# Rewriting a one-core decode-layer forward and backward kernel: program order, 32-bit transposes, longer DMA rows

## The chip, the cores and the metric

The kernel runs on one NeuronCore of a Trainium2 chip. The metric is device time in microseconds (us) of one execution, as the median of several runs. TensorE (PE) multiplies matrices into PSUM, VectorE (DVE) and ScalarE (ACT) copy PSUM to SBUF and do elementwise work, GpSimd (POOL) and SyncE (SP) mostly issue DMAs. Sixteen DMA engines move data between HBM and SBUF; SP, ACT and POOL each issue onto a queue of their own, and all three queues share the sixteen engines.

## The reference

One decode step (batch 4, one query token, model width 512): attention over a sliding window of a K/V cache (32 query heads, 8 K/V heads, head size 128, cache length 4096, window the last 1024 positions) and a gated FFN (width 1792), both from the layer-normed input, and all gradients. Cut to what matters:

```python
W = max(256, Sk // 4)                              # 1024 of 4096 positions
q = (xn @ wq) ; k = k_cache[:, :, Sk-W:] ; v = v_cache[:, :, Sk-W:]
o = softmax(q k^T * Dh**-0.5) v
y = x + o @ wo + (gelu(xn @ w_gate) * (xn @ w_up)) @ w_down
out, vjp = jax.vjp(f, x, k_cache, v_cache, wq, wo, w_gate, w_up, w_down)
return out, *vjp(grad_out)
```

All data are bf16. The gradients of the two caches are 32 MiB each, and three quarters of each is zero (the positions outside the window); these zeros must be written too. Queries in a group of 4 heads share one K/V head, and there is one token per batch, so every product of activations is thin: the large operands are weights and K/V blocks, most of which are wanted transposed.

## The kernel before

The eight K/V heads are handled in four groups `t` of two heads (`GP = 2`). For each group the kernel

- `pre`: transposes `wo` (128x128 bf16 blocks, eight to a PSUM tile, line 258, copied out by DVE on line 92) and forms the output gradient and the queries of its eight query heads by products with 4 moving columns;
- `scores(t, 0)` and `scores(t, 1)`: transposes K, then V, block by block (`T_ps`, line 306), copies them to `T_sb`, and multiplies (`S_ps`, line 311) with four products side by side in 32-column groups of the array (`tile_position`);
- `softmax`, `softmax_d`: the softmax and its derivative;
- `odq`: the attention output and the gradient of q (`od_ps`, line 377);
- `dvdk`: the gradients of V and K as outer products with a contraction of 32 (`kv_ps`, line 406), cast into a staging tile `stg`, and stored;
- `dw`: the gradients of `wo` and `wq`; `fin`: transposes `wq` and adds the group's part of the output and of dx to `acc`.

The FFN comes first, with the same parts: transposes (`wdT_ps`, `wgT_ps`), thin products, and gradients (`dwd_ps`, `dwg_ps`) that are cast into `osb_d` and `osb_g`.

Products whose result is only stored are put into a list `bg` and popped a few at a time by `tick(n)`, between other work. `evac` (lines 91 and 92) gives each PSUM evacuation to ACT or DVE by a running cost balance; bf16 blocks of transposes go to DVE always. The tile framework schedules all engines except SP itself; only SP's queue keeps program order (`manual_schedule(engines={nc.sync.engine})`). PSUM has one pool of four buffers (`ps_w`) for all transposes and products.

DMA: the FFN weights, the first group and part of the second are loaded on SP, the rest on ACT (lines 206, 208, 213). K and V rows: the 1024 positions are split as 128 partitions x 8 positions, so that one descriptor row is 8 x 128 bf16 = 2 KB. `zeros()` issues all 32 zero stores (1536 KB each, 6 KB rows) on SP directly behind its loads; each waits until the one two before it has landed. All gradients are stored from POOL (line 96).

Of the kernel before, what the change touches and what calls it, by code (L numbers as in the profile page):

```python
# [13 lines left out]
BF16 = mybir.dt.bfloat16  # L14
P = 128
# [3 lines left out]
def kernel(  # L19
# [34 lines left out]
    ND = D // P  # L54
    NF = F // P
    J = W // P
# [3 lines left out]
    RG = B * HG  # L60
    NQ = P // RG
    WQ = W // NQ
    JQ = J // NQ
    NS = B * GP
    CW = HG * Dh
    assert Sq == 1 and Dh == P and D == 512 and F % P == 0 and RG == 32 and JQ * NQ == J and WQ == JQ * P
    scale = float(Dh) ** -0.5
    eps = 1e-5

    const = ctx.enter_context(tc.tile_pool(name="const", bufs=1))  # L70
    kvp = ctx.enter_context(tc.tile_pool(name="kvp", bufs=3))
    wres = ctx.enter_context(tc.tile_pool(name="wres", bufs=2))
    attw = ctx.enter_context(tc.tile_pool(name="attw", bufs=2))
    tsb = ctx.enter_context(tc.tile_pool(name="tsb", bufs=5))
    outp = ctx.enter_context(tc.tile_pool(name="outp", bufs=3))
    ps_w = ctx.enter_context(tc.tile_pool(name="ps_w", bufs=4, space=bass.MemoryType.PSUM))
    ps_a = ctx.enter_context(tc.tile_pool(name="ps_a", bufs=1, space=bass.MemoryType.PSUM))
    ps_x = ctx.enter_context(tc.tile_pool(name="ps_x", bufs=1, space=bass.MemoryType.PSUM))
    ctx.enter_context(tc.manual_schedule(engines={nc.sync.engine}))

    load = {"act": 0.0, "dve": 0.0}

    def evac(out, in_, n, half=False, eng=None):

        eng = "dve" if half else eng
        ca, cd = (190 + n) / 1.2, (120 + (n / 2 if half else n)) / 0.96
        if eng is None:
            eng = "act" if load["act"] + ca <= load["dve"] + cd else "dve"
        load[eng] += ca if eng == "act" else cd
        if eng == "act":  # L90
            return nc.scalar.copy(out=out, in_=in_)  # L91
        return nc.vector.tensor_copy(out=out, in_=in_)  # L92

    def store(eng, out, in_, kind, apart):

        d = eng.dma_start(out=out, in_=in_)  # L96
        for k in apart:
            tc.declare_no_dep(d.ins, group=k, reason="stores write disjoint parts of the outputs")
        tc.add_to_no_dep_group(kind, d.ins)
        return d  # L100


    RB = P // B
    x_b = const.tile([P, D], BF16, name="x_b")
    dy_b = const.tile([P, D], BF16, name="dy_b")
    for dst, src in ((x_b, A_x), (dy_b, grad_out)):
        nc.sync.dma_start(out=dst[:], in_=bass.AP(tensor=src.tensor, offset=src.offset,
                                                  ap=[[D, B], [0, RB], [1, D]]))

# [3 lines left out]
    nc.vector.tensor_copy(out=ident_f[:], in_=ident[:])  # L113
    one_f = const.tile([1, 1], FP32, name="one_f")
    nc.vector.memset(one_f[:], 1.0)

    msk_i = const.tile([P, rep], FP32, name="msk_i")
    nc.vector.reduce_sum(out=msk_i[:], in_=ident_f[:].rearrange("p (b r) -> p r b", b=B)[:, 0:rep, :], axis=AX.X)


    rsum = const.tile([P, NQ, RG], FP32, name="rsum")
    nc.gpsimd.memset(rsum[:], 1.0)

    msk_f = const.tile([P, GP, B], FP32, name="msk_f")
    nc.gpsimd.memset(msk_f[:], 1.0)
    for q in range(NQ):
        rs = slice(q * RG, (q + 1) * RG)
        nc.gpsimd.affine_select(out=rsum[rs], in_=rsum[rs], pattern=[[0, NQ], [-1, RG]],
                                compare_op=ALU.is_equal, fill=0.0, base=0, channel_multiplier=1)
        nc.gpsimd.affine_select(out=msk_f[rs], in_=msk_f[rs], pattern=[[-rep, GP], [-HG, B]],  # L130
                                compare_op=ALU.is_ge, fill=0.0, base=0, channel_multiplier=1)
        nc.gpsimd.affine_select(out=msk_f[rs], in_=msk_f[rs], pattern=[[rep, GP], [HG, B]],
                                compare_op=ALU.is_ge, fill=0.0, base=rep - 1, channel_multiplier=-1)
    msk = const.tile([P, GP, B], BF16, name="msk")
    nc.vector.tensor_copy(out=msk[:], in_=msk_f[:])

    ZW = K0 // P * Dh
    ztile = const.tile([P, ZW], BF16, name="ztile")
    nc.vector.memset(ztile[:], 0.0)

    qm_all, dom_all = [], []
    for i in range(2):
        for lst, nm in ((qm_all, "qm"), (dom_all, "dom")):
            t_ = const.tile([P, NS, RG + rep], BF16, name=f"{nm}{i}")
            nc.gpsimd.memset(t_[:], 0.0)
            lst.append(t_)


    acc = const.tile([P, 2, ND, B], FP32, name="acc")
    nc.vector.memset(acc[:], 0.0)  # L150

    def acc_add(o, ps):
        nc.vector.tensor_tensor(out=acc[:, o], in0=ps, in1=acc[:, o], op=ALU.add)

    def acc_sum(o, terms):

        ps = ps_w.tile([P, ND, B], FP32, name="acc_ps", tag="w")
        for c in range(ND):
            for k, (lf, rhs) in enumerate(terms):
                nc.tensor.matmul(ps[:, c, :], lhsT=lf(c), rhs=rhs, start=(k == 0), stop=(k == len(terms) - 1))  # L160
        acc_add(o, ps[:])


    od_ps = ps_a.tile([P, 2, GP, Dh], FP32, name="od_ps")
    nc.vector.memset(od_ps[:], 0.0)


    stats = const.tile([P, nc.vector.BN_STATS_DIM], FP32, name="stats")
    nc.vector.bn_stats(out=stats[:], in_=x_b[:])
    mv = const.tile([P, nc.vector.BN_AGGR_DIM], FP32, name="mv")  # L170
    nc.vector.bn_aggr(out=mv[:], in_=stats[:])
    eps_t = const.tile([P, 1], FP32, name="eps_t")
    nc.vector.memset(eps_t[:], eps)
    rstd = const.tile([P, 1], FP32, name="rstd")
    nc.scalar.activation(out=rstd[:], in_=mv[:, 1:2], func=ACT.Sqrt, bias=eps_t[:], scale=1.0)
    nc.vector.reciprocal(out=rstd[:], in_=rstd[:])
    xn_f = const.tile([P, D], FP32, name="xn_f")
    nc.vector.tensor_scalar(out=xn_f[:], in0=x_b[:], scalar1=mv[:, 0:1], scalar2=rstd[:, 0:1],
                            op0=ALU.subtract, op1=ALU.mult)
    xn_b = const.tile([P, D], BF16, name="xn_b")  # L180
    nc.vector.tensor_copy(out=xn_b[:], in_=xn_f[:])

    xnT = const.tile([P, ND, B], BF16, name="xnT")
    dyT = const.tile([P, ND, B], BF16, name="dyT")
    for src, dstT in ((dy_b, dyT), (xn_b, xnT)):
        tps = ps_x.tile([P, ND, P], BF16, name="tps", tag="x")
        for c in range(ND):
            nc.tensor.transpose(tps[:, c, :], src[:, c * P:(c + 1) * P], ident[:])
        nc.vector.tensor_copy(out=dstT[:], in_=tps[:].rearrange("p c (b r) -> p c b r", b=B)[:, :, :, 0])


    xnm = const.tile([P, rep, D], BF16, name="xnm")
    dym = const.tile([P, rep, D], BF16, name="dym")
    for src, dst in ((dy_b, dym), (xn_b, xnm)):
        for i in range(rep):
            nc.vector.tensor_scalar(out=dst[:, i, :], in0=src[:], scalar1=msk_i[:, i:i + 1], scalar2=None,
                                    op0=ALU.mult)


    wo_v = A_wo.rearrange("(t h p) n -> t p h n", p=P, h=HG)  # L200
    wq_v = A_wq.rearrange("(c p) (t j) -> t p c j", p=P, j=CW)
    wo_t, wq_t, k_t, v_t = {}, {}, {}, {}

    def load_w(t, eng):
        wo_t[t] = wres.tile([P, HG, D], BF16, name="wo_sb", tag="wo")
        eng.dma_start(out=wo_t[t][:], in_=wo_v[t])
        wq_t[t] = wres.tile([P, ND, CW], BF16, name="wq_sb", tag="wq")
        eng.dma_start(out=wq_t[t][:], in_=wq_v[t])  # L208

    def load_kv(t, k, g, eng):  # L210
        d_, src, nm = ((k_t, A_k_cache, "kb"), (v_t, A_v_cache, "vb"))[k]
        tl = kvp.tile([P, B, J, Dh], BF16, name=nm, tag=nm)
        eng.dma_start(out=tl[:].rearrange("p b j d -> p b (j d)"),  # L213
                      in_=src[:, t * GP + g, K0:Sk, :].rearrange("b (m j) d -> m b (j d)", j=J))
        d_[(t, g)] = tl

    def load_next(t, k):

        if t + 1 < NT:
            load_kv(t + 1, k, 1, nc.scalar)  # L220
        if t + 2 < NT:
            load_kv(t + 2, k, 0, nc.scalar)


    ZG = 2
    zlist = [(og, b, g) for b in range(B) for g in range(0, G, ZG) for og in (out_2, out_3)]

    def zeros():
# [14 lines left out]
    def tick(n):  # L243
        for _ in range(min(n, len(bg))):
            bg.popleft()()


    st = {}

# [462 lines left out]
```

## Time and profile before

| | |
|---|---|
| median of 3 runs | 313.86 us (311.71 to 315.93) |
| span of the profiled execution | 311.7 us |
| PE, weight loads | 224.1 us busy (72%), 144.7 us (46%) |
| DVE | 146.3 us (47%) |
| ACT | 113.4 us (36%) |
| POOL | 51.3 us (16%) |
| data moved | 112.38 MB: 30.93 MB read from HBM, 81.01 MB written |
| mean rate over the span | 361 GB/s |

The span is the time from the first to the last instruction of one profiled execution, and its length equals the lowest of the three runs. Busy time of PE is modelled from pipelined instructions. "Mean ns" of a matmul is its latency, and busy time divided by the count is what it costs in a row of its like.

### The profile page before, as it was taken

To read this page: it belongs to the slowest core of one execution; us is meant where nothing else is said; L and a number is where in the kernel's file an instruction comes from. 1 tells how busy PE (TensorE), PEld (TensorE's weight loads), DVE (VectorE), ACT (ScalarE), POOL (GpSimd) and SP (SyncE) were. 2 spreads that over 40 slices of the span, in tenths; PEclk is the share of its full clock that TensorE was granted. 3 is DMA by queue.
4 is the path that set the end of the run, shared out by engine and by line. 5 is a ranking of instruction groups with operands and counts; after the bars stand their busy time and mean duration, and the time that the engine had idled before them with its cause. 6 is when DMAs were issued, how large, how long until landed. Compare 5 with 4: busy or idle time off the path is not lost.

```text
span 311.7 us, 6831 instructions
## 1 busy us (share of the span) xinstructions
PE 224.1 (72%) x2950; PEld 144.7 (46%) x2956; DVE 146.3 (47%) x304; ACT 113.4 (36%) x217; POOL 51.3 (16%) x76
## 2 busy tenths in 40 slices
PE   1269986936988379779648069969789755979861
PEld 0259874615555244465425044455556333756231
DVE  5246663523743234537414025546545424564766
ACT  3010645613613045346022044435244414533650
POOL 6000121610100005201000004201000501110140
PEclk9998998875975555779955555679955559895585
DMA  5999999999999999999999999998999999431494
GB/s 167 397 351 385 374 402 416 416 422 424 419 295 392 418 374 418 421 420 419 375 418 414 357 418 416 421 420 346 394 410 405 418 422 418 159 145 62 181 335 160
DMA packets 34405, 112.38 MB, mean 361 GB/s; under 512 B 1664, under 2 KB 7816, under 8 KB 34376
## 3 DMA queue, kind: packets, MB, share of 16 engines
q1 hardware_dynamic: 18136, 66.59, 53.6%
q0 software_dynamic: 7808, 30.67, 24.8%
q10 hardware_dynamic: 8432, 14.69, 13.6%
q8 instruction: 23, 0.38, 0.5%
q14 instruction: 6, 0.05, 0.0%
HBM read 30.93 MB, written 81.01 MB: 359 GB/s over the span
## 4 chain that ended last, share of the span: by engine, by line
PE 39%; DMA 30%; ACTq 9%; DVE 8%; issue 6%; ACT 4%; POOL 1%; SPq 1%; DVEq 0%; POOLq 0%
PE T_ps L306 11%; DMA kb<-in_A_k_cache_dram 10%; PE kv_ps L406 7%; ACTq L208 6%; DMA wd_sb<-in_B_w_down_dram 6%; DMA out_dram<-osb_o 5%; DMA vb<-in_A_v_cache_dram 5%; PE S_ps L311 4%; ACTq L213 3%; DMA out_dram<-osb_d 3%; DMA out_dram<-osb_g 2%; PE dwo_ps L426 2%; PE wgT_ps L619 2%; PE wdT_ps L546 2%; PE wqT_ps L471 2%
## 5 line engine op out<-in xcount | busy, mean ns | idle before, releaser
L92 DVE COPY T_sb<-T_ps 128x1024 bf16<-128x1024 bf16 x64 | 44.2, 691 | 41.5 <-PE T_ps L306 40.9
L91 ACT CAST stg_dk<-kv_ps 128x512 bf16<-128x512 f32 x46 | 25.0, 590 | 47.0 <-issue 26.9
L91 ACT CAST stg_dv<-kv_ps 128x512 bf16<-128x512 f32 x52 | 28.2, 590 | 31.9 <-PE kv_ps L406 22.7
L306 PE MATMUL T_ps<-ident,kb 128*128 128x128 bf16 x256 | 32.9, 280 | 6.1 <-DMA kb<-in_A_k_cache_dram 5.0
L406 PE MATMUL kv_ps<-qmr,dS_b 32*128 32x512 bf16 x64 | 23.1, 598 | 16.9 <-ACT stg_dk L91 16.4
L306 PEld LDWEIGHTS <-kb 128*128 128x128 bf16 x256 | 23.0, 125 | 22.2 <-issue 13.3
L306 PE MATMUL T_ps<-ident,vb 128*128 128x128 bf16 x256 | 26.6, 242 | 0.2
L406 PE MATMUL kv_ps<-domr,P_b 32*128 32x512 bf16 x64 | 18.6, 476 | 5.9 <-DVE wqT L92 3.0
L306 PEld LDWEIGHTS <-vb 128*128 128x128 bf16 x256 | 19.0, 109 | 8.0 <-issue 4.8
L91 ACT CAST osb_g<-dwg_ps 128x384 bf16<-128x384 f32 (+1 forms) x30 | 14.4, 534 | 17.2 <-DMA out_dram<-osb_g 5.9
L92 DVE COPY woT<-woT_ps 128x1024 bf16<-128x1024 bf16 x16 | 11.1, 691 | 20.2 <-PE woT_ps L258 20.2
L92 DVE CAST stg_dk<-kv_ps 128x512 bf16<-128x512 f32 x18 | 12.1, 686 | 16.8 <-PE kv_ps L406 16.6
L258 PEld LDWEIGHTS <-wo_sb 128*128 128x128 bf16 x128 | 11.4, 127 | 17.5 <-issue 17.2
L91 ACT CAST osb_o<-dwo_ps 128x512 bf16<-128x512 f32 x23 | 12.8, 587 | 17.1 <-PE dwo_ps L426 15.3
L91 ACT CAST osb_q<-dwq_ps 128x512 bf16<-128x512 f32 x25 | 13.6, 589 | 13.8 <-PE dwq_ps L441 9.2
L92 DVE COPY wqT<-wqT_ps 128x1024 bf16<-128x1024 bf16 x16 | 11.1, 691 | 15.7 <-PE wqT_ps L471 15.7
L96 POOL DMA_DIRECT2D out_dram<-stg_dv x8 | 6.0, 754 | 72.9 <-ACT stg_dv L91 41.8
L258 PE MATMUL woT_ps<-ident,wo_sb 128*128 128x128 bf16 x128 | 15.5, 285 | 1.3 <-DVE stg_dk L92 0.8
L471 PEld LDWEIGHTS <-wq_sb 128*128 128x128 bf16 x128 | 11.1, 129 | 10.5 <-issue 10.5
L471 PE MATMUL wqT_ps<-ident,wq_sb 128*128 128x128 bf16 x128 | 14.8, 287 | 0.8 <-DVE stg_dv L92 0.8
L96 POOL DMA_DIRECT2D out_dram<-stg_dk x8 | 6.1, 767 | 54.6 <-ACT stg_dk L91 42.5
L91 ACT CAST osb_d<-dwd_ps 128x512 bf16<-128x512 f32 x14 | 8.1, 586 | 14.3 <-PE dwd_ps L580 13.4
(182 smaller groups left out, 349.3 us busy)
## 6 DMA issues: line engine op xcount, KB each, us to landing
out_dram<-ztile SPq DMA_DIRECT2D x32, 1536.0 KB, 11.2
out_dram<-stg_dv POOLq DMA_DIRECT2D x8, 1024.0 KB, 11.5
out_dram<-stg_dk POOLq DMA_DIRECT2D x8, 1024.0 KB, 12.4
vb<-in_A_v_cache_dram ACTq DMA_DIRECT2D x5, 1024.0 KB, 15.8
kb<-in_A_k_cache_dram ACTq DMA_DIRECT2D x5, 1024.0 KB, 26.0
out_dram<-osb_o POOLq DMA_DIRECT2D x8, 512.0 KB, 10.4
out_dram<-osb_q POOLq DMA_DIRECT2D x8, 512.0 KB, 4.7
out_dram<-osb_g POOLq DMA_DIRECT2D x8, 448.0 KB, 7.4
```

What stands on the lines that cost most here:

```text
L91: return nc.scalar.copy(out=out, in_=in_)
L92: return nc.vector.tensor_copy(out=out, in_=in_)
L96: d = eng.dma_start(out=out, in_=in_)
L208: eng.dma_start(out=wq_t[t][:], in_=wq_v[t])
L213: eng.dma_start(out=tl[:].rearrange("p b j d -> p b (j d)"), in_=src[:, t * GP + g, K0:Sk, :].rearrange("b (m j) d -> m b (j d)", j=J))
L258: nc.tensor.transpose(wT_ps[:, i, c, :], wo_sb[:, 2 * h2 + i, c * P:(c + 1) * P], ident[:])
L306: nc.tensor.transpose(T_ps[:, j, :], blks[(t, g)][:, b, j, :], ident[:])
L311: nc.tensor.matmul(ps[q * RG:(q + 1) * RG, :], lhsT=lf[:, s * RG:(s + 1) * RG], rhs=T_sb[:, q * WQ:(q + 1) * WQ], start=(g == 0 and b == 0 ...
L406: nc.tensor.matmul(mps[:].rearrange("p b d -> p (b d)"), lhsT=src[rs, jj * P:(jj + 1) * P], rhs=mr[rs, g].rearrange("p b d -> p (b d)"), s ...
L426: nc.tensor.matmul(mps[:], lhsT=o_r[:, g, :], rhs=dym[:, i, :], start=True, stop=True)
L471: nc.tensor.transpose(wT_ps[:, i, c, :], wq_sb[:, c, h * Dh:(h + 1) * Dh], ident[:])
L546: nc.tensor.transpose(wT_ps[:, i, c, :], wd_sb[:, 2 * f2 + i, c * P:(c + 1) * P], ident[:])
```

## The change

The file is rewritten almost entirely; the computation is the same. Its parts:

1. **Program order.** `manual_schedule()` covers all engines. Each `step` issues four transposes and one DVE copy, one stage of a softmax or FFN chain written as a generator, and two items of `bg`, with larger products put in by hand as `mid`. PSUM: two buffers for transposes (`ps_t`), two for `bg` products (`ps_b`), four single ones.
2. **32-bit transposes.** Pairs of bf16 are viewed as one fp32, so that a 128x128 transpose moves 256 bf16 columns. The result holds even and odd columns interleaved; later products read one of the two with a stride of two elements. 480 such transposes stand in place of 936 bf16 ones.
3. **Rows.** A partition holds 32 positions of one batch, so K/V rows are 8 KB in loads and stores. Rows of the weights, and of most weight gradients, become 4 to 14 KB by interleaving (`wq` and its gradient keep 2 KB).
4. **Array groups.** Thin products with 4 moving columns become products with 32 or 64 stationary columns side by side in column groups; `kv_ps` uses a contraction of 64 in two row groups instead of 32 in four, with the same count of 128.
5. **Evacuation.** Transposes are copied by DVE. All `bg` casts are on ACT until the last group is done; then ACT and DVE alternate (`turn["mix"]`).
6. **DMA queues.** All loads go to SP, the next group's while this one is worked on (V into a single buffer at the group's end). The zeros go to ACT's queue, 12 KB rows from 64 partitions, one at a time in the order of the steps (`zplan`); six are left to the end. A tiny memset or copy stands before each store on POOL or ACT.

```diff
-    ctx.enter_context(tc.manual_schedule(engines={nc.sync.engine}))
+    ctx.enter_context(tc.manual_schedule())
...
-        for og, b, g in zlist:
-            z = store(nc.sync, og[b, g:g + ZG, 0:K0, :].rearrange("g (m j) d -> m g (j d)", m=P), zsrc, "zeros",
-                      ["rest"])
+    def zeros(n):
+        for _ in range(min(n, len(zq))):
+            og, b, g = zq.popleft()
+            store(nc.scalar, og[b, g:g + ZG, 0:K0, :].rearrange("g (m j) d -> m g (j d)", m=64), zsrc, "zeros")
...
+    zplan = {12: 1, 16: 1, 20: 1, 24: 1} | {28 + 4 * i: 1 for i in range(22)}
+    def step(work, mid=None, n=2):
+        work()
+        advance()
+        tick(n // 2)
+        if mid is not None:
+            mid()
+        tick(n - n // 2)
+        zeros(zplan.get(where["n"], 0))
+        where["n"] += 1
+    def t4(blocks, out, perm):
+        ps = ps_t.tile([P, 4, P], FP32, name="T_ps", tag="t")
+        np_, wd = blocks[0].shape
+        for i, blk in enumerate(blocks):
+            nc.tensor.transpose(ps[0:wd, i, 0:np_], blk, ident_f[0:np_, 0:np_])
+        nc.vector.tensor_copy(out=out, in_=perm(ps[0:wd, :, 0:np_]))
...
+    for t in range(NT + 1):
+        if t < NT:
+            for k in range(4):      # mid of k=0: score_mms(t-1, 1, 1), start softmax_d(t-1)
+                step(lambda: wo_chunk(t, k), mid)
+            heads(t)
...
+        if t > 0:
+            for k in range(4):      # mids: heads_T(t); flush, odq(t-1, 1); dw(t-1)
+                step(lambda: wq_chunk(t - 1, k), mid)
+            fin_T(t - 1)
...
+        for k in range(2):
+            for g in range(GP):
+                for ch in range(4): # mids: fin(t-1), loads(t+1), score_mms, start softmax(t)
+                    step(lambda: kv_chunk(t, k, g, ch), mid)
+        flush_chains()
+        odq(t, 0)
+        if t + 1 < NT:
+            load_kv(v_t, A_v_cache, "vb", t + 1, kv0)
+    fin(NT - 1)
...
+    tick(len(bg))
+    zeros(len(zq))
```

There are 24 steps in the FFN, 20 for the first group, 24 for each of the other three, and 4 behind the last.

## The prediction

> **What bounds the kernel now.** I read the table of 40 slices first, because it shows where the limit changes. Each slice is 7.8 us; the rows are DMA busy in tenths, GB/s, and the granted TensorE clock.
>
> ```profile
> PEclk9998998875975555779955555679955559895585
> DMA  5999999999999999999999999998999999431494
> GB/s 167 397 351 385 374 402 416 416 422 424 419 295 392 418 374 418 421 420 419 375 418 414 357 418 416 421 420 346 394 410 405 418 422 418 159 145 62 181 335 160
> ```
>
> From 8 us to about 265 us the DMA engines are full, at some 400 GB/s; in the last six slices they move 62 to 335 GB/s. So there are two kernels in sequence: one bound by transfers, and an uncovered tail. The totals by stage say the same (columns: stretch, length, busy us of PE, PEld, DVE, ACT, POOL with counts, granted clock, DMA share, GB/s):
>
> ```profile
> 50.00:110.00 60.00, 41.95 (x555) 26.90 (x558) 25.18 (x51) 21.20 (x44) 9.04 (x11) 0.72 1.01 400
> 222.00:265.00 43.00, 32.05 (x384) 19.89 (x370) 17.87 (x35) 15.49 (x30) 7.54 (x7) 0.64 1.02 411
> 265.00:312.00 47.00, 34.24 (x409) 20.01 (x407) 28.21 (x53) 20.67 (x38) 7.62 (x10) 0.72 0.46 172
> ```
>
> Why there is a tail: the queue of SP in order of time, and the chain of waits between 222 and 253 us (start, length, what).
>
> ```profile
> 38.91 217.96 SPq L96 DMA_DIRECT2D out_dram<-ztile  x32
> ```
> ```profile
> 222.29 30.32 DMA kb<-in_A_k_cache_dram
> ```
>
> The zeros, 50.3 MB of no urgency, are pressed through between 39 and 257 us, always two in flight. They compete with loads: the last K block is asked for at 222.3 us and lands 30.3 us later. The whole last group then stands behind it, 252.7 to 311.7 us, with nothing left for the DMA engines but its own 6 MB. No engine is at its limit even there (PE 34 of 47 us); it is the group's dependent chain. The transfers set 257 us, the uncovered group the rest.
>
> **The change, part by part.**
>
> *Bytes and rows.* Bytes stay at about 112 MB. Packets fall from 34405: zeros from 8192 rows of 6 KB to 4096 of 12 KB, K/V from 2 KB to 8 KB. What this is worth is read from the queues:
>
> ```profile
> q1 hardware_dynamic: 18136, 66.59, 53.6%
> q0 software_dynamic: 7808, 30.67, 24.8%
> q10 hardware_dynamic: 8432, 14.69, 13.6%
> ```
>
> Bytes by engine time: q10 (mean row 1.7 KB) 14.69 MB / (0.136 x 311.7 us x 16) = 21.7 GB/s per engine, q0 (3.9 KB) 24.8, q1 (3.7 KB) 24.9. Longer rows are faster, with less gain the longer they are. The nearest rows for a stage of long rows are the best slices, 418 to 424 GB/s; the stages as a whole give 400 to 411. I take 412: 112 / 0.412 = 272 us of transfers, between 264 (424) and 280 (400).
>
> A page rule speaks against the whole part: the Trainium skill, "DMA: Bandwidth & Descriptors", Specifications, gives a limit of some 358 GB/s of HBM for a core. By it 112 MB would take 313 us and no rewrite could gain; the slices above hold 416 to 424 GB/s for many us, so the measurement decides, and the sum goes without the rule.
>
> *Transposes.* 936 bf16 transposes go, 480 of 32 bits come. The profile of before has eight 128x128 fp32 transposes (the final `f_ps`): min, median, max in ns, first and last start.
>
> ```profile
> L658 PEld LDWEIGHTS f_ps<-ident_f,acc_r x8: 138/140/143, 304.2 to 304.9; 128*128 128x128 f32 x8
> L658 PE MATMUL f_ps<-ident_f,acc_r x8: 272/272/328, 304.2 to 305.0; 128*128 128x128 f32 x8
> ```
> ```profile
> L306 PE MATMUL T_ps<-ident,kb 128*128 128x128 bf16 x256 | 32.9, 280 | 6.1 <-DMA kb<-in_A_k_cache_dram 5.0
> ```
>
> 272 ns against 280, and 1.09 us for the eight (0.136 each) against 32.9/256 = 0.129 each: one fp32 transpose costs as much as one bf16 transpose and does twice the data. PE saves about 456 x 0.12 = 55 us busy. None of it is on the path while DMA is full; in the tail it is worth something.
>
> A second rule is against it: "TensorE: Matmul & The Clock Gate", Weight-path perf modes, excludes fp32 from the fast weight load. The weight load of the row above, 140 ns, is 0.01 to 0.03 us above the bf16 ones; by the rule's factor of about 2 it would be an estimated 0.1 us more for each transpose. The sum uses the row.
>
> DVE copies the same bytes, 128x512 fp32 instead of 128x1024 bf16: 120 copies (before 117) at 0.69 us (both forms show 0.68 to 0.69), no change. Thin products: 848 of four moving columns at 0.036 us (30 us, lines 160, 263, 268, 500, 551, 624) become 288 wide ones in column groups. The `od_ps` rows (512 in 10.3 us, 0.02 each) show four groups at once; a 512-column product by itself costs 0.43 (`dwo_ps`). Between them 12 to 60 us; the form is that of `od_ps`, so 15. Nothing on PE is a bound by itself: 224 - 55 - 15 = 154 us. Reading with a two-element stride has no row; from nothing to twice the `S_ps` products (21 us), I take nothing.
>
> *Program order and the pace of a group.* This is the risky part. In a full step ACT makes two casts at 0.59 us, and each fourth step issues a zero (0.37 us by its SP rows) and a small copy (0.2): 2 x 0.59 + 0.15 = 1.33 us, 24 steps 32 us. DVE needs 24 x 0.69 + about 11 = 28 us, PE about 30, mostly beside ACT. The `mid` products run on PE while ACT drains, since two PSUM buffers hold only 1.2 us of casts: scores 64 x 0.083 = 5.3, `odq` 64 x 0.04 = 2.6, `heads` and `fin` 1.3 + 2.6 by `od_ps` (up to 20 by `dwq_ps` and `dwo_ps`), hops about 1.2: 13 (to 28). So X = 45 us a group, bounds 40 to 60. The one row for a whole group: the last group of before took 252.7 to about 304, 51 us, with its chain uncovered.
>
> *Stages by program order.* FFN: the third weight lands at 20.8 us in before; 16 steps of 0.69 on DVE, 11 chain operations of about 0.62, and hops and a table load of 4 give 43; 48 casts behind (16 x 0.59 + 32 x 0.53 = 26, some 4 of it covered) give 65 (57 to 73). First group, without casts: 30. Three groups 3 x 45 = 135. End: 48 casts shared by two engines 15, the last derivative and products 10: 25. All compute done at 255. Only then ACT issues the last six zeros: 9.4 MB / 0.42 = 22.5, landing 2: **279.5 us**.
>
> *Transfers in these stages:* FFN 11.8 MB of loads, 3 zeros of 1.57 and 5.5 of gradients, 22 MB (53 of 65 us); first group 5 zeros and 4.2 of loads, 12 MB (29 of 30); groups two and three 6 zeros, 6.3 of loads and 6.3 of gradients, 22 MB each (53.5 of 45); the last 18 MB (43), end 6.3 MB (15 of 25). The excess of 2 x 8.5 carries over in the queues; group four and the end absorb 12, 5 remain: **284.5**. Cross-check from the other side: 272 + 4.6 for the slow first 8 us + 6 idle in the FFN + 2 = 284.6.
>
> *New waits.* A zero on ACT waits, by the framework's eight DMA semaphores, for a transfer about eight earlier. Behind it in ACT stand the casts, behind these PE (two PSUM buffers) and everything. Eight in flight are some 10 MB, 25 us, more than the backlog of 17, so I cost it at nothing; if the cover goes, the ACT stall is in X. The loads on SP have nothing behind them; ACT loses the stalls that loads cost it (8.8 us at 101 us in the chain). V of the next group is asked for 12 steps before its use, 16 us or more, for 2.1 MB: 15 us at a third of the rate. If it is late, each group pays a few us.
>
> Span 284.5; before, the median stood 2.2 us above the profiled span of 311.7, so I forecast **286 us**.
>
> **Rivals.**
>
> *The pace of the in-order engines becomes the bound* (slower). End = 144.5 + 3X. For: two PSUM buffers, all casts on ACT, an ACT that waits for DMAs, 51 us for the one uncovered group seen. Against: that group had 128 K/V transposes instead of 64 and no next group to fill its chain. X = 50 gives 294; from X = 53.7 the gain is under 2% and from 57.8 the kernel is slower by 2%; at 62, 331 us.
>
> *The transfers keep the old rate and overlap worse*: 280 + 4.6 + 12 + 2 = 299. For: stages held 400 to 411, not 424, with reads and writes mixed. Against: rows are longer.
>
> *Everything overlaps*: 264 + 4.6 + 2 + 2 = 273 with the median. For: best slices. Against: six zeros held behind all compute.
>
> *The 32-bit transposes cost four passes*: 96 x 0.4 a group, X above 75, 370 us. The `f_ps` row is against it.
>
> **How the numbers follow.** Two per cent is about what a measurement of this kernel tells from no change: 307.6 to 320.1 us. Chances: the forecast (278 to 293) 0.46, full overlap 0.12, old rate 0.19, pace-bound with X of 53.7 to 57.8 0.10, slower pace 0.11, four passes 0.02. Faster 0.77, same 0.10, slower 0.13. The range leaves out a little of full overlap below 271 and the slow cases above 313.
>
> **What would show it.** Right: DMA tenths at 9 up to the end but for slices around 35 to 65 us; no SP or ACT load stall in the chain; zeros last in the chain, ending it for some 22 us; T_ps rows of fp32 at about 0.13 us each; groups of 45 to 53 us. Wrong: low DMA tenths inside groups, ACT idle behind a DMA named as releaser, a chain of PE and ACT casts, or rates below 400 GB/s with the engines full.

## The result and the profile after

The changed kernel is slower: a median of 326.5 us (323.09 to 329.17, four runs) against 312.78 us (311.61 to 315.93, four runs) of the kernel before, a ratio of 1.037 with a 95% interval of 1.027 to 1.048. The profiled execution took 326.89 us with a span of 325.2. (Ratios here and below leave disturbed runs out, so they need not equal the quotient of the medians.)

The table of 40 slices, 8.1 us each (granted TensorE clock in tenths of full speed, rate of the DMA engines):

```profile
PEclk9997555655699999999789999659699959555555
GB/s 207 392 411 419 219 306 307 58 320 424 362 360 399 194 381 403 357 422 423 432 418 421 430 425 421 428 420 426 425 377 420 402 25 257 4 210 275 426 429 339
```

The middle is what the prediction wanted: from slice 17 to 31 (138 to 260 us) the DMA engines are full, mostly above 418 GB/s. But there are now two holes, not one: 33 to 65 us, and 260 to 298 us; behind the second hole the engines are full again, for 27 us in which nothing is computed. The totals by stage, cut where the program's stages change (stretch, length, busy us of PE, PEld, DVE, ACT, POOL with counts, granted clock, DMA share, GB/s):

```profile
0.00:34.00 34.00, 19.82 (x131) 12.77 (x131) 25.12 (x51) 6.34 (x10) 9.93 (x26) 0.92 0.96 361
34.00:54.80 20.80, 19.81 (x65) 9.35 (x68) 5.70 (x10) 10.87 (x22) 1.73 (x4) 0.50 0.71 275
54.80:63.20 8.40, 8.40 (x54) 1.78 (x54) 0.24 (x1) 2.13 (x4) 0.65 (x2) 0.52 0.12 48
63.20:81.70 18.50, 10.47 (x27) 2.42 (x26) 0.00 (x0) 11.14 (x23) 1.24 (x5) 0.58 0.98 363
81.70:110.30 28.60, 24.66 (x256) 17.55 (x257) 20.93 (x34) 5.91 (x18) 0.61 (x2) 0.91 0.79 326
110.30:159.00 48.70, 43.38 (x403) 25.44 (x404) 32.11 (x53) 32.63 (x67) 3.78 (x12) 0.99 1.00 395
159.00:213.00 54.00, 40.88 (x383) 24.72 (x383) 27.22 (x45) 28.74 (x59) 3.83 (x12) 0.88 1.01 424
213.00:254.00 41.00, 37.31 (x333) 22.27 (x336) 19.94 (x35) 24.14 (x50) 3.79 (x12) 0.83 0.99 413
254.00:298.30 44.30, 30.90 (x171) 11.28 (x163) 28.32 (x46) 13.09 (x24) 3.03 (x10) 0.69 0.44 180
298.30:325.20 26.90, 0.00 (x0) 0.00 (x0) 0.00 (x0) 0.95 (x6) 0.72 (x1) 0.50 0.93 390
```

Beside the forecast's stages:

| stage | forecast | measured |
|---|---|---|
| FFN, until its last cast | 65 | 81.7 |
| first group | 30 | 28.6 |
| the three other groups, until the last `odq(t, 0)` (forecast: 135 and 5 of backlog) | 140 | 143.7 |
| end of compute | 25 | 44.3 |
| six zeros behind it | 24.5 | 26.9 |
| sum | 284.5 | 325.2 |

Of the 40.7 us, 36 are lost at the two ends: 16.7 in the FFN and 19.3 in the end. Read as transfers, 112 MB at the 424 GB/s of the best stage are 264 us, and the other 61 us of the span are unused rate. In a stretch of length L with rate r that loss is L x (1 - r/424). The end of compute loses 25 us, 34 to 63 us loses 15, the first group 7, the first 34 us 5, and all others together some 9.

The issues of the zeros (shortest, median and longest in ns, start of the first and the last), and the three longest transfers in the chain of waits (start, length, what):

```profile
L100 ACTq DMA_DIRECT2D out_dram<-ztile x32: 607/608/1405, 28.7 to 303.4; - x32
```
```profile
67.90 9.86 DMA out_dram<-osb_g
...
128.04 33.89 DMA wq_sb<-in_A_wq_dram
...
176.03 40.06 DMA wq_sb<-in_A_wq_dram
```

Two loads of 34 and 40 us stand in the chain. They look like the disease and are not: in both stages the engines moved 395 and 424 GB/s, so a late load there is the backlog of transfers that the forecast priced. The transfer that costs something is the first, in a stage with holes on either side.

### The profile page after: what moved, and what is told of

The parts are those of the page before. It is cut to its first block, busy times and chain, and to the rows that moved or that the text cites. A ratio compares the mean times of both kernels' runs of the same rounds, so it can differ in the third digit from the quotient of the medians.

```text
span 325.2 us, 4433 instructions
## 1 busy us (share of the span) xinstructions
PE 235.6 (72%) x1801; PEld 127.6 (39%) x1801; DVE 159.6 (49%) x273; ACT 135.9 (42%) x279; POOL 29.3 (9%) x85
## 4 chain that ended last, share of the span: by engine, by line
PE 44%; DMA 26%; DVE 17%; ACT 4%; issue 2%; ACTq 1%; POOL 0%; SPq 0%; POOLq 0%; DVEq 0%
DMA wq_sb<-in_A_wq_dram 23%; PE T_ps L286 13%; PE kv_ps L615 7%; PE acc L238 4%; DMA out_dram<-osb_g 3%; PE SP_ps L519 3%; PE od_ps L596 2%; PE dwg_ps L399 2%; PE dwd_ps L387 2%; DVE woT L287 2%; DVE T_sb L287 2%; ACT osb_g L90 2%; PE dwq_ps L644 1%; ACTq L100 1%; DVE stg_dk L89 1%
## 5 line engine op out<-in xcount | busy, mean ns | idle before, releaser
L287 DVE COPY T_sb<-T_ps 128x512 f32<-128x512 f32 x64 | 43.7, 690 | 37.1 <-PE T_ps L286 36.5
L90 ACT CAST stg_dk<-kv_ps 128x512 bf16<-128x512 f32 x56 | 31.0, 587 | 24.9 <-PE kv_ps L615 24.5
L287 DVE COPY woT<-T_ps 128x512 f32<-128x512 f32 x16 | 17.1, 1087 | 29.8 <-PE T_ps L286 29.8
L615 PE MATMUL kv_ps<-Rm,dSm 64*128 64x512 bf16 x64 | 25.1, 432 | 5.5 <-DVE stg_dk L89 4.3
L90 ACT CAST osb_g<-dwg_ps 128x448 bf16<-128x448 f32 x32 | 15.9, 533 | 18.4 <-PE dwg_ps L399 11.1
L615 PE MATMUL kv_ps<-Rm,Pm 64*128 64x512 bf16 x64 | 21.9, 388 | 0.9 <-DVE stg_dv L89 0.6
L286 PE MATMUL T_ps<-ident_f,kb 128*128 128x128 f32 x128 | 21.6, 297 | 0.9 <-DVE T_sb L287 0.9
L286 PEld LDWEIGHTS T_ps<-ident_f,kb 128*128 128x128 f32 x128 | 14.5, 147 | 12.6 <-issue 8.5
L286 PE MATMUL T_ps<-ident_f,vb 128*128 128x128 f32 x128 | 19.3, 276 | 0.0
L286 PEld LDWEIGHTS T_ps<-ident_f,vb 128*128 128x128 f32 x128 | 15.3, 142 | 6.9 <-issue 3.5
L519 PE MATMUL SP_ps<-T_sb,z 128*64 128x256 bf16 x256 | 17.8, 278 | 0.0
```

Source lines behind the costliest of these rows:

```text
L286: nc.tensor.transpose(ps[0:wd, i, 0:np_], blk, ident_f[0:np_, 0:np_])
L287: nc.vector.tensor_copy(out=out, in_=perm(ps[0:wd, :, 0:np_]))
L519: nc.tensor.matmul(SP[jq * 64:(jq + 1) * 64, k, :], lhsT=z[:, e, s * 64:(s + 1) * 64], rhs=T[:, b, e, jq * n:(jq + 1) * n], start=(g == 0 ...
L615: nc.tensor.matmul(ps[:].rearrange("p g d -> p (g d)"), lhsT=src[rs, jj].rearrange("p m b -> p (m b)"), rhs=st[t][("dom", "qm")[k]][rs, :] ...
```

## The experiments

Three theories were set against each other at first. **A**: the two ends lose it; the middle groups go at the pace of the transfers. **B**: PE is the pace everywhere, because the 32-bit transposes are dearer than forecast. **C**: program order on all engines costs it. All kernels below compute the whole output.

**e1_T_twice**: each 32-bit transpose is issued twice into the same place.

```diff
         for i, blk in enumerate(blocks):
-            nc.tensor.transpose(ps[0:wd, i, 0:np_], blk, ident_f[0:np_, 0:np_])
+            for _ in range(2):
+                nc.tensor.transpose(ps[0:wd, i, 0:np_], blk, ident_f[0:np_, 0:np_])
```

> The changed kernel with each of its 480 fp32 transposes issued twice into the same PSUM place; the output is the same. Each costs 0.15 us at full clock and 0.25 at half (four in 0.60 and 1.03 us in the changed kernel's profile), so PE gets 71 to 120 us more work. Theory A (the time was lost at the two ends, in the FFN and behind the last K/V block, while the groups between are paced by transfers): groups two to four hide most of theirs, the FFN, the first group and the end show theirs; 350 to 365 us. Theory B (PE sets the pace everywhere, since it is busy 236 us where 154 were forecast): 395 us or more. Theory C (the fixed order of each engine is what costs, whatever the work): as A.

340.8 us (two runs), ratio to the kernel before 1.087 (1.073 to 1.101). Only 14 us came for 480 further transposes, below what any of the theories had expected. The clocks, and the stages of groups two and three:

```profile
PEclk9999757955999999999999999969999969655555
```
```profile
112.00:160.00 48.00, 47.06 (x475) 33.49 (x474) 26.59 (x44) 28.10 (x58) 3.31 (x11) 1.00 0.89 333
160.00:216.00 56.00, 55.05 (x559) 38.62 (x557) 31.38 (x51) 32.29 (x67) 4.31 (x14) 1.00 1.01 425
```

PE is shown busy 47 of 48 and 55 of 56 us, yet the groups grew by little: from one `od_b` (the gradient of a group's output, once a group) to the next it is 48.9 and 52.9 us, against 47.3 and 54.2 in the changed kernel. A "busy" PE had room. But part of this is cover: the 47.3 us hold 7.4 of idle time for a load, the 48.9 of e1 1.2. So the 48.9 us are the engines' own pace with the added work, 4.8 above the 44.1 that f4 shows below without it. The clock, which rose from 0.79 to 0.86 in the mean with the added work, may be a part of the small price. B falls as stated; PE is close to the limit inside a group, but it doesn't make the 41 us.

**e2_zeros_end**: the six last zeros are issued in the last steps instead of behind everything.

```diff
-    zplan = {12: 1, 16: 1, 20: 1, 24: 1} | {28 + 4 * i: 1 for i in range(22)}
+    zplan = {12: 1, 16: 1, 20: 1, 24: 1} | {28 + 4 * i: 1 for i in range(22)} | {n: 1 for n in range(114, 120)}
```

> The changed kernel with the six zero stores that it keeps for after all casts issued in steps 114 to 119 instead, where the last group ends and the DMA engines fall to 180 GB/s. Theory A: the 27 us behind the last cast shrink to the landing of the last gradients, so 300 to 306 us. Theory B: the same stores have room there too, but what they gain is lost where they stand in ACT's queue before casts; 310 to 326. Theory C: as A.

313.8 us (ten runs), ratio 0.994 (0.989 to 0.999): some 13 us less than the changed kernel, half of what theory A had expected and inside the range of B. Where the other half went, by stage:

```profile
260.00:280.00 20.00, 15.09 (x92) 5.41 (x92) 8.20 (x12) 2.59 (x7) 1.22 (x4) 0.50 1.01 427
280.00:305.00 25.00, 16.16 (x31) 3.67 (x30) 14.34 (x24) 8.44 (x15) 1.81 (x6) 0.50 0.60 252
```

The zeros fill the DMA engines from 260 to 280 us, but compute now ends at 305 instead of 298 and is itself the last thing: 25 us at clock 0.50 in which no engine is busy more than two thirds. So the zeros behind compute hid that the end of compute is too long, and moving them into it made it longer: from the last group's `od_b` to the last cast it is 80.1 us in the changed kernel and 89.3 here (216.0 to 305.3).

**e3_sched**: only SP keeps program order, as in the kernel before.

```diff
-    ctx.enter_context(tc.manual_schedule())
+    ctx.enter_context(tc.manual_schedule(engines={nc.sync.engine}))
```

> The changed kernel with all its work, but with only SP in program order, as in the kernel before; the framework orders PE, DVE, ACT and POOL. Theory A: the FFN and the end stay bound by two PSUM buffers and one engine of casts, so within 4% of 326 us, either way. Theory B: no change, PE has the same work. Theory C: 295 us or less, since a free order fills the gaps at both ends.

354.1 us (347.9 to 354.4, four runs). Without program order this text is slower: its fastest run is 19 us above the slowest of the changed kernel. No theory had this number (A had within 4% of 326, C 295 or less); the direction is against C, which falls for this text.

**e4_before_inorder**: the other way round, all engines of the kernel *before* in program order (with a tiny memset before each store on POOL, as in the change).

```diff
-    ctx.enter_context(tc.manual_schedule(engines={nc.sync.engine}))
+    ctx.enter_context(tc.manual_schedule())
...
+        if eng is nc.gpsimd:
+            eng.memset(gap_p[:], 0.0)
         d = eng.dma_start(out=out, in_=in_)
```

> The kernel before with all engines in program order (and a tiny memset ahead of each store on POOL, which such an order needs). Its text was not written for this: softmax and odq stand behind whole stretches of transposes. Theory C: well above 326 us, since program order is the cost of the change. Theory A: the transfers of the middle keep most of it covered, 315 to 335 us. Theory B says nothing of it.

416.7 us (two runs), ratio 1.330 (1.312 to 1.347). By its number this is what C expected: program order costs a text that isn't written for it about 100 us (with the memsets, which weren't tried alone). The changed kernel, whose steps are written for it, is 90 us below; how much of that the steps do, and how much the other parts of the change, isn't shown.

The next three were made on e2, to take the two ends apart.

**f2_nomix**: the end's casts are all on ACT.

```diff
-            turn["mix"] = True
```

> The kernel with the six zeros issued in steps 114 to 119, and all casts of the end on ACT, as in the rest of it, none on DVE. Theory A: sharing the casts between two engines buys nothing while two buffers run in step (1.36 us a pair against 2 x 0.59 on ACT alone), and DVE's own chain for dx no longer stands in front of casts: 2 to 8 us less, 306 to 312. Were the casts the limit, as the forecast had it (48 casts at 0.3 us): 10 us more, 323.

306.0 us (four runs), ratio 0.973 (0.967 to 0.979): one engine is *faster* than two, by some 7 us (the ratios of e2 and f2 are 0.021 apart). In time order, the changed kernel's casts in its end, and below them f2's (start, length, engine, line, operation, idle before):

```profile
288.33 1.01 PE L635 MATMUL dwo_ps<-dy_r,om 128*128 128x512 bf16 x2 [0.36 <-DVE osb_o L89]
...
288.95 0.69 DVE L89 CAST osb_o<-dwo_ps 128x512 bf16<-128x512 f32 x1 [0.68 <-PE dwo_ps L635]
289.38 0.58 ACT L90 CAST osb_o<-dwo_ps 128x512 bf16<-128x512 f32 x1 [0.78 <-PE dwo_ps L635]
289.69 1.01 PE L635 MATMUL dwo_ps<-dy_r,om 128*128 128x512 bf16 x2 [0.35 <-DVE osb_o L89]
```
```profile
278.30 1.08 PE L635 MATMUL dwo_ps<-dy_r,om 128*128 128x512 bf16 x2 [0.18 <-ACT osb_o L90]
278.92 1.08 ACT L90 CAST osb_o<-dwo_ps 128x512 bf16<-128x512 f32 x2 [0.18 <-PE dwo_ps L635]
279.56 1.08 PE L635 MATMUL dwo_ps<-dy_r,om 128*128 128x512 bf16 x2 [0.18 <-ACT osb_o L90]
```

Two pieces take 1.36 us shared (288.33 to 289.69) and 1.26 us on ACT alone (278.30 to 279.56). With two PSUM buffers the second engine buys nothing: both sit idle for 0.7 to 0.8 us in each pair, because PE waits for both buffers and they for PE. But 0.1 us in each of 12 pairs is only about 1 us. Most of the rest stands in DVE's queue: each second cast waits there behind the serial chain for dx, from 272.0 to 278.9 us. Just behind that chain, in the changed kernel:

```profile
278.21 0.68 DVE L768 TENSOR_TENSOR dx_b<-tb,dy 4x512 bf16<-4x512 f32 x1
278.82 1.27 DVE L89 CAST stg_dk<-kv_ps 128x512 bf16<-128x512 f32 x2
...
279.54 2.55 PE L615 MATMUL kv_ps<-Rm,dSm 64*128 64x512 bf16 x4 [3.34 <-DVE stg_dk L89]
...
280.16 0.58 ACT L90 CAST stg_dk<-kv_ps 128x512 bf16<-128x512 f32 x1 [4.38 <-PE kv_ps L615]
```

PE sits idle for a buffer that DVE holds, and ACT for PE. In f2 ACT casts through that chain; compute ends at about 288 us, 18 before e2's, and the engines move 426 GB/s through the whole end:

```profile
252.50:288.00 35.50, 27.79 (x135) 9.16 (x134) 12.53 (x23) 22.39 (x46) 3.18 (x11) 0.73 1.01 426
```

Only part of the 18 us shows in the time, because 15 us of transfers still stand behind compute. And part of them is what e2 itself had lost: from the last group's `od_b` to the last cast f2 takes 71.4 us, e2 89.3, the changed kernel 80.1.

**f1_tail4**: casts shared as in e2, but the products of the end take four PSUM buffers, the two of the transposes as well.

```diff
+    def pb4(shape, name):
+        turn["p"] = turn.get("p", 0) + 1
+        if turn.get("four") and turn["p"] // 2 % 2:
+            return ps_t.tile(shape, FP32, name=name + "2", tag="t")
+        return ps_b.tile(shape, FP32, name=name, tag="b")
...
-            ps = ps_b.tile([P, D], FP32, name="dwo_ps", tag="b")
+            ps = pb4([P, D], "dwo_ps")
...
+    turn["four"] = True
     fin(NT - 1)
```

> The kernel with the six zeros issued in steps 114 to 119, and from the last fin on the products of gradients take turns between four PSUM buffers (the two of ps_t beside the two of ps_b). In its profile two pieces take 1.36 us (one product 0.60, one DVE cast 0.69, both buffers in step), 25 pieces 17 us. Theory A (the ends are bound by two PSUM buffers): with four, ACT and DVE run side by side at about 0.35 us a piece, so 7 to 8 us less, 305 to 307. Theory B (PE sets the pace, here at half clock, 0.43 us a product): 0.43 a piece, 5 to 6 us less, 308. If neither the casts nor PE are the end: 313.

304.5 us (four runs), ratio 0.967 (0.960 to 0.974): some 8 us less than e2 by the ratios.

**f3_ffn4**: the same in the FFN: behind its last step, casts shared by both engines over four buffers.

```diff
+        turn["mix"] = turn["four"] = True
         flush_chains()
...
         tick(ffn_bg)
+        turn["mix"] = turn["four"] = False
```

> The kernel with the six zeros issued in steps 114 to 119, and the FFN's casts behind its last step shared by ACT and DVE and given four PSUM buffers. In its profile the products behind the last step run from 54.8 to 82 us, 10 us of which ACT waits for stores of osb_g. Theory A: 27 pieces at 0.3 instead of 0.57 would save 7 us, but the stores still have to land before a buffer is free; 3 to 7 us less, 307 to 311. Theory B: PE at half clock gives 0.43 a piece, 2 to 4 us less. If the store's wait takes all of it: 313.

308.1 us (four runs), ratio 0.983 (0.974 to 0.992): some 3 us less than e2 by the ratios, whose intervals overlap. The first `od_b` comes at 80.8 us, in e2 at 88.4; this is the clearer sign.

**f4_all**: the changed kernel with f1's and f3's buffers together, and the zeros put where the engines have room, densely through the FFN and the first group, sparsely through the full groups.

```diff
-    zplan = {12: 1, 16: 1, 20: 1, 24: 1} | {28 + 4 * i: 1 for i in range(22)}
+    zplan = {n: 1 for n in (12, 14, 16, 18, 20, 21, 22, 23, 24, 27, 30, 33, 36, 39, 42, *range(45, 111, 6), 113,
+                            115, 116, 117, 118, 119)}
```

> Four PSUM buffers and shared casts at both ends, and the 32 zeros moved to where the DMA engines were idle: eight in steps 12 to 23 of the FFN, eight in the first group, eleven in the three groups between, five at the end. Theory A: FFN 77, first group 30, the groups between no longer paced by 22 MB of transfers each but by about 45 us of their own, end 40: 285 to 298 us, faster than both kernels. Theory B: the groups between keep 48 to 54 us, since PE paces them: 300 to 308.

294.0 us (290.3 to 296.4, four runs), ratio 0.926 (0.917 to 0.934). It beats both kernels. The rate in its slices of 7.2 us, and `od_b` of groups two to four:

```profile
GB/s 195 373 404 416 431 363 374 378 419 406 395 395 429 425 429 430 417 420 383 383 424 423 429 422 423 403 431 417 429 421 427 425 412 421 322 430 404 14 345 237
```
```profile
116.23 0.39 ACT L471 ACTIVATE od_b<-oq_ps 128x256 bf16<-128x256 f32 x1 [1.37 <-PE oq_ps L468]
160.33 0.39 ACT L471 ACTIVATE od_b<-oq_ps 128x256 bf16<-128x256 f32 x1 [1.37 <-PE oq_ps L468]
204.38 0.39 ACT L471 ACTIVATE od_b<-oq_ps 128x256 bf16<-128x256 f32 x1 [1.36 <-PE oq_ps L468]
```

The hole of the FFN is filled, and that of the end but for the last 22 us. With fewer zeros in them the groups go at 44.1 us each, two intervals that agree to 0.1, with 1.4 us of idle time before the line and no load in the chain: that is the engines' own pace, X. In the changed kernel the same line comes at intervals of 47.3 and 54.2 us, with idle time of 7.4 and 13.6 us before it: there the transfers set the pace. The FFN still shows its wait: ACT has no free `osb_g` until a store lands, and that store stands in the chain for 12.2 us now. So f4 hides that hole, it doesn't close it.

**g2_loads1**: on e2, the next group's loads are issued in the first group's first step instead of ahead of it, to find out whether they are what delays that store.

```diff
-    loads(1)
     for t in range(NT + 1):
...
+                mid = (lambda: loads(1)) if (t, k) == (0, 0) else None
```

> The kernel with the six zeros issued in steps 114 to 119 (313.8 us), with the loads of the second group (4.2 MB) issued in the first step of the first group instead of ahead of it. In its profile they start at 63 us and ACT then waits 10 us for stores of osb_g to land. If the loads' competition is what delays those stores, the FFN ends 5 to 8 us earlier and the time is 306 to 309; if the stores are late for another reason (they are issued late and the two buffers are few), 313.

313.3 us (ten runs), ratio 1.006 (0.999 to 1.012), and the store is still 9.0 us of the chain. The first `od_b` came 2.2 us earlier (86.2 us), the time did not: the loads are at most a small part of that wait.

**g3_best**: f4 with g2's edit, and two of its zeros between the last casts.

```diff
-    zplan = {n: 1 for n in (..., 113, 115, 116, 117, 118, 119)}
+    zplan = {n: 1 for n in (..., 113, 116, 118, 119)}
...
-    tick(len(bg))
+    tick(6)
+    zeros(1)
+    tick(6)
+    zeros(1)
+    tick(len(bg))
     zeros(len(zq))
```

> The kernel with four PSUM buffers and shared casts at both ends and the zeros moved into idle stretches (294.0 us), with the second group's loads issued in the first group and two of the last zeros issued among the last casts, where the DMA engines fall to 14 GB/s for one slice. If these are the remaining gaps: 284 to 290. If the wait for osb_g is set by the zeros now standing in the FFN: 291 to 295.

299.9 us (294.3 to 306.4, six runs), ratio 0.951 (0.943 to 0.959): not better than f4 but slower, by the two ratios some 8 us, and outside both expected ranges. The store of `osb_g` stands in its chain for 14.7 us; the rest of the loss stays open.

Two runs asked what the long rows and the timing of the zeros do in the kernel before.

**e5_before_z12k**: its zeros as 12 KB rows from 64 partitions. For the room, `T_sb` gets three buffers instead of four.

```diff
-    ZW = K0 // P * Dh
+    ZW = K0 // 64 * Dh
...
-            z = store(nc.sync, og[b, g:g + ZG, 0:K0, :].rearrange("g (m j) d -> m g (j d)", m=P), zsrc, "zeros",
+            z = store(nc.sync, og[b, g:g + ZG, 0:K0, :].rearrange("g (m j) d -> m g (j d)", m=64), zsrc, "zeros",
```

> The kernel before with its zeros alone in 12 KB rows from 64 partitions (and one buffer of T_sb fewer, to make room for the longer source). This is the row part of the change for 45% of the bytes. By the forecast, rows of 6 KB to 12 KB are worth about 3% of 50 MB, 3 to 4 us of the 257 us in which the DMA engines are full, 309 to 312 us. If the higher rate of the changed kernel's middle (424 GB/s against 400 to 411) comes from the zero rows, 8 us or more: 306. If the three T_sb buffers cost more than the rows gain: above 315.

339.4 us (four runs), ratio 1.077 (1.070 to 1.084). SP's waits point away from the rows themselves: SP's queue, in which the zeros are, now stands behind V loads for 89.0 us and behind one store for 44.6, where the kernel before had 22.5 us of the first kind and none of the second; the DMA engines meanwhile fall to 64 and 148 GB/s in two slices. Which of the edit's sides moved these waits (a buffer fewer, or the order of DMA semaphores) was not tried apart, so the run says nothing of what the rows are worth in time. What it does say is the price of a row: the packets of 12 KB in its trace take 460 ns in the median, those of 6 KB in the kernel before 234, a gain of 1.7% a byte.

**e6_before_z1**: one zero in flight instead of two.

```diff
-            if len(done) >= 2:
-                tc.add_manual_dep(z.ins, done[-2].ins.name,
+            if len(done) >= 1:
+                tc.add_manual_dep(z.ins, done[-1].ins.name,
```

> The kernel before with one zero store in flight at a time instead of two, nothing else. It tests the reading of its profile on which the forecast stood: the zeros starve the loads, the last K block lands 30 us after its issue, and a whole group is left uncovered behind. By it the loads land earlier, the zeros reach into the last group, and the time falls to 290 to 305 us. If the tail is the group's own chain whatever the zeros do: 308 to 316. If one store in flight cannot fill the DMA engines: above 318.

315.9 us (ten runs), ratio 1.006 (1.002 to 1.009). By its number this is the branch "the group's own chain whatever the zeros do". The trace says otherwise. The last instruction of compute, in the kernel before and in e6, and SP's longest wait in e6 (for what, us in total, times, longest):

```profile
308.36 0.69 DVE L680 TENSOR_TENSOR dx_b<-pr,dy_b 128x512 bf16<-128x512 f32 x1
```
```profile
296.92 0.69 DVE L680 TENSOR_TENSOR dx_b<-pr,dy_b 128x512 bf16<-128x512 f32 x1
...
SPq L96 <- DMA out_dram<-ztile: 251.3, 31, 16.4
```

K loads on ACT's queue land in 18.9 us instead of 26.0 (medians), and all compute is done 11 us earlier. But the zeros, each waiting for the one before, have become a chain of their own, from 39 to 308 us, mostly at 330 to 390 GB/s where there had mostly been 400 to 420. They now end the kernel, at about the time at which compute had ended it. So the first half of the reading holds, that the zeros delayed the loads and with them the last group; a single zero in flight is the wrong remedy for it.

The end's 19 us were still not split up. Two last runs took sharing out by itself.

**h2_after_nomix**: the changed kernel, with nothing but `turn["mix"] = True` taken out.

> The changed kernel with nothing else edited than that its last casts stay on ACT instead of taking turns with DVE. With the zeros moved, the same edit brought the last cast from 300 to 284 us. Theory A (the forecast's 25 us for the end were missed because a shared cast, two PSUM buffers and DVE's own dx chain run in step): the end falls from 44 to about 30 us with the six zeros still behind it, 310 to 314 us. If the earlier gain hung on where the zeros stood: 322 to 327.

321.2 us (318.5 to 327.9, four runs), ratio 1.020 (1.009 to 1.031): about 5 us less than the changed kernel, with intervals that overlap, and short of the 310 to 314 us that theory A gave.

**h1_all_nomix**: f4's zeros and FFN, with the end's casts on ACT alone over two buffers (f4 without `turn["mix"] = True` and `turn["four"] = True` in the end).

> The kernel with four PSUM buffers and shared casts behind the FFN's last step and the zeros moved into idle stretches (294.0 us), but with the end's casts on ACT alone with two buffers. Theory A: the end takes some 30 us from the last odq(t, 0) on, as with the six zeros moved; there the four shared buffers took 40: 282 to 288. If with four buffers the end was no longer bound by the casts: 292 to 296.

291.3 us (284.4 to 293.7, four runs, no interval): not to be told from f4. Here one engine over two buffers does as well as two over four.

## Why the prediction was wrong

**What bounds the kernel before: right as far as e6 tests it.** With the zeros held back the loads land earlier and the last group, and all compute with it, ends 11 us earlier. The time didn't fall, because zeros in single file take until 308 us. What an order of zeros between the two would bring that kernel wasn't tried.

**The middle: right in size.** X was forecast at 45 us, f4 shows 44.1; transfers of groups two and three were forecast at 53.5 us each, and the groups took 47.3 and 54.2; the first group took 28.6 us for 30, the last zeros 26.9 for 24.5; stages of long rows held 395 to 424 GB/s for a forecast 412. The working behind X was less good than its sum: it had PE busy about 30 us beside ACT, and f4 has PE busy 42 of these 44 us. e1 puts twice the transposes into a group and gets 48.9, so the 44 are not PE's limit in a strict sense.

**The transposes: wrong, and with little weight.** The step "one fp32 transpose costs as much as one bf16 transpose" compared a row at granted clock 1.00 (`f_ps`, at 304 us) with one averaged over stages at 0.64 to 0.83. At equal clock, in the changed kernel's own chain, four fp32 blocks against eight bf16 blocks (`pT_ps`), the same bytes:

```profile
90.73 0.67 PE T_ps L286 x4
...
164.92 0.64 PE pT_ps L533 x8
...
261.96 1.05 PE pT_ps L533 x8
...
266.21 1.04 PE T_ps L286 x4
```

The first two are in slices of clock 0.8 and more, the others in one of 0.5: a byte costs the same both ways. So the saving of 55 us isn't there, and PE has 235.6 us busy, not 154. Here the Trainium skill, "TensorE: Matmul & The Clock Gate", Weight-path perf modes, had spoken against the step and was set aside for the row: its fast weight load leaves fp32 out, and the estimate from it, 0.1 us more for each transpose, was of the right size (0.67/4 against 0.64/8 us). That the weight load is the reason isn't shown: its rows (medians of 140 ns here, 98 for the bf16 V blocks of the kernel before) differ by 0.04 us, half of that. That the saving is missing cost little by itself, to judge by e1, which doubles the transposes for 14 us.

**The FFN (65 forecast, 81.7 measured): the term that was mis-sized at the front.** Its chain of vector work was done at about 35 us, but with eight of the 16 steps still to come; the forecast's 43 us counted all 16, and the last copy ended at 55.0. The step that failed is "48 casts behind" (26 us, some 4 of it covered). From 34 us on they took 48 us, of which ACT casts for 24. The lines from 34 to 81.7 us above show the other 24 by ACT's idle time: 9.9 us in the eight steps and 6.3 in the products into `acc`, while PE, at a clock of 0.50 to 0.52, is busy 28 of 29 us and ACT waits for it through two buffers; then 7.4 around a store of `osb_g` (9.9 us in the chain). The forecast had counted casts by ACT's duration alone, no PE at half clock, no `acc` products, and no wait for a store. f3 shows that sharing with more buffers brings back 7.6 us of it. g2 shows that the loads of the next group are at most a small part of what holds the store; the rest of its cause stays open. How much the half clock itself costs stays open: in e1 parts of this stage ran at full clock with twice the transposes, and it ended 2.4 us later.

**The end (25 forecast, 44.3 measured): the term that was mis-sized most.** Two steps failed. "48 casts shared by two engines 15" took half of ACT's time for each piece; measured, a shared pair takes 1.36 us, 0.68 a piece, more than one cast of ACT (0.58). And "the last derivative and products 10" is a chain of some 25 us by itself: to the last `od_ps` at 265.7, `acc` to 271.6, and DVE's dx chain to 278.9. Then come 19 us of casts that should have been beside it. The chain's last attention products and its last products into `acc`, in the changed kernel:

```profile
263.78 1.90 PE od_ps L596 x32
...
270.60 1.04 PE acc L238 x13
```

f2 (7 us), f1 (8) and h1 agree that casts through that chain, on ACT or over more buffers, are what is missing, with the zeros issued before the end. h2, f2's edit with the zeros still behind, brought about 5 us, which the intervals can't tell from 7 or from nearly nothing. How the 19 us split between sharing, buffers and PE at half clock (0.50 from 278.9 us on) isn't settled.

**Zeros behind all compute: right in size, but it is what turned the rest into time.** Each us that compute ran late moved 9.4 MB of transfers back by one us. The engines stood idle for 25 us' worth just ahead of them. The cross-check from the side of the transfers, 272 + 4.6 + 6 + 2, could not warn of this: against the 264 us of a full rate it allows 20 us of unused rate, and took the length of the FFN from the very term that was short; 61 us were measured.

**The rivals.** "The pace of the in-order engines" had the right sign, and its formula gives the measured span at X = 60.2. But the runs put the loss elsewhere: X is 44.1. It was a rival about the steady state, and the ends had none. Four passes of the transposes, the old rate and the full overlap didn't happen.

**The new waits: right for the zeros, not for the loads.** No cast waits for zeros in the chain. The last zeros' issues on ACT stretch to 1.4 us, with nothing behind them. But the forecast let the excess of transfers carry over in the queues without a wait, and took a load in the chain as a sign of being wrong: two `wq` loads of 34 and 40 us stand there, and ACT is idle for 7.4 and 13.6 us until the products behind them are there. The DMA engines are full meanwhile, and the three groups together came out only 3.7 us above the forecast.

## What to carry to other kernels

Forecast the first and the last stage on their own, as chains with PSUM round trips at the clock of that stage, and not as a count of casts by their duration: here all of the middle came out right and both ends came out short, by 17 and 19 us. Transfers that can go at any time belong where the engines have holes, and not behind the last compute, where they turn every late us into time; f4 won 10% on the changed kernel so, together with more buffers at the ends. Here a second engine for evacuation paid only with buffers for it, and it must have nothing of its own in front.

## What was not expected of the hardware

- More work on PE raised its granted clock. With each transpose issued twice, the mean went from 0.79 (0.782 to 0.791 in four runs) to 0.86 (0.859 in both runs), and some slices of the FFN from 0.5 to 0.7 and 0.9: 480 more transposes cost 14 us. The mean can move without an edit too: e4's two runs, of one kernel and within 3 us, had 0.71 and 0.89.
- Rows of 12 KB are 1.7% cheaper a byte than rows of 6 KB (medians of 460 ns and 234 ns a packet), 8 KB (309, changed kernel) against 2 KB (84) 8%. The rate of a full stage, 424 GB/s, is what the kernel before already had in its best slices.
